# Last-64-row items of an attention and spectral-mix kernel moved from the end to the middle of the tail

## The chip, the cores and the metric

One Trainium2 chip, one of its cores. The metric is device time in microseconds. The kernel before took 428.51 us as the median of 7 runs (427.82 to 429.5). Beside these there is one profiled execution, which took 429.14 us; the instructions that the profile shows span 427.4 us of it. All times below with one or two decimals and no other source are places in that span, counted from its start.

## What is computed

Eight batches, eight heads, 576 positions and head size 64. Four heads use a local causal window of 32 positions, four a strided mask. The attention result, read as 576 rows of 512 columns per batch, then goes through a spectral mix and a residual layer:

```python
scores = np.where(masks[None], scale * np.matmul(q, k.transpose(0, 1, 3, 2)), -1e9)
attn = softmax(scores)
x = np.matmul(attn, v)                       # then laid out as (8, 576, 512)
X = np.fft.rfft(x, axis=1)
Yr = einsum('bmd,mde->bme', Xr, w_r) - einsum('bmd,mde->bme', Xi, w_i)   # 64 modes
Yi = einsum('bmd,mde->bme', Xr, w_i) + einsum('bmd,mde->bme', Xi, w_r)
u = x + np.fft.irfft(Yr + 1j * Yi, n=S, axis=1)
return u + np.maximum(u @ w_ch, 0.0)         # (8, 576, 512) in float32, 9.44 MB
```

## The kernel before, in words

The first two stages do attention (strided heads, then local heads), with the spectral products of the 64 modes woven in while their weights stream in from HBM. The weights come through transfers that the GpSimd queue issues (line 186), and that stream fills most of the span. The program writes the order of the instructions out by hand: each engine executes its instructions in the order of the code.

The change lies in the tail, which begins once the last weights have landed (about 391 us). The output is produced there by 18 *items*. An item is a pair (batches, t). For t from 0 to 3 it holds two batches and, of each, 128 rows of the output (every second row of the first 256 or of the next 256 rows). For t = 4 it holds four batches and, of each, the last 64 rows (512 to 575); the first batch of each pair lies on partitions 0 to 63 of a tile, the second on partitions 64 to 127. Every item has 512 KB of output. In the kernel before, items 0 to 15 have t < 4, and items 16 and 17 are the two with t = 4 (line 976).

For each item k the tail does, in this order:

- `v_early(k)` (line 987): two matmuls with the identity bring the kept product of the residual layer into PSUM. `u_early(k)` (line 992) does the same with the kept rows.
- `new_rows` (line 1001): matmuls over 32 rows that add what the last spectral group brings, from `zzs` to the v half and from `yys` to the u half. An item with t < 4 takes two of them for each half, an item with t = 4 takes four, each for 64 rows.
- `v_done(k)` (line 1013): ScalarE writes the ReLU of the v half to `rl`.
- `u_done(k)` (line 1020): VectorE adds the u half and `rl` into an output tile `osb`. Then a transfer stores it: at line 1028, one for an item with t < 4, on the queue of SyncE; at line 1031, one for each batch of an item with t = 4, also on SyncE's queue, except that odd batches of the last item are stored from ScalarE's queue.

The loop at line 1067 runs the v half of item k beside the u half of item k-1. At k = 8 it first runs `spec_z(3, 1, held)` (line 736), four matmuls whose result `zzs[1]` the items with batches 4 to 7 need, and a copy of it by ScalarE. `pieces(k)` cuts the ReLU, the addition and the store of item 0 in two. `osb` tiles rotate over five buffers, those that held the weights. PSUM has three two-bank buffers `p` and one `u`; an even item's u half uses `p`, an odd one's `u`.

Of the kernel before, what the change touches and what calls it, by code (L numbers as in the profile page):

```python
# [56 lines left out]
def kernel(  # L57
# [10 lines left out]
    nc = tc.nc  # L68
# [17 lines left out]
    def psum(kind, half=False, pair=False):  # L86
        if pair:
            return pss[kind].tile([128, 2, 512], FP, tag=kind, name=kind)
        if half:
            return pss[kind].tile([128, 1024], F16, tag=kind, name=kind)  # L90
        return pss[kind].tile([128, 512], FP, tag=kind, name=kind)
# [146 lines left out]
    def normalise(val, den, n, pieces, dst):  # L238
        rec = pin.tile([128, 8], FP, tag="rec", bufs=4, name="rec")
        nc.vector.reciprocal(out=rec[0:n, 0:pieces], in_=den)  # L240
        nc.vector.tensor_tensor(  # L241
            out=dst,
            in0=val.rearrange("p h (q c) -> p h c q", c=4),
            in1=rec[0:n, 0:pieces]
            .to_broadcast((n, pieces, 64))
            .rearrange("p h (q c) -> p h c q", c=4),
            op=AluOp.mult,
        )

    def act_copy(out, in_):  # L250
        nc.scalar.activation(out=out, in_=in_, func=ACTF.Copy)  # L251
# [481 lines left out]
    def spec_z(g, bq, zp):  # L733
        for e in range(4):
            lhs = YS["YT"][:, e, g, ds(8 * bq, 8), :].rearrange("p x m -> p (x m)")
            nc.tensor.matmul(
                zp, lhs, w_chs["n"][:, e, :], start=(e == 0), stop=(e == 3)
            )
# [228 lines left out]
    for n, i in enumerate([3, 5, 7] + list(range(8, 21))):  # L967
        b, t = n // 2, n % 2 * 2
# [4 lines left out]
    items = []  # L973
    for P0 in (0, 2):
        items += [((2 * P, 2 * P + 1), t) for t in range(4) for P in (P0, P0 + 1)]
    items += [(range(b, b + 4), 4) for b in (0, 4)]
    LAST = len(items) - 1
    vps, ups, rls, osbs = {}, {}, {}, {}

# [4 lines left out]
    def v_early(k):  # L984
        vps[k] = psum("p", pair=True)
        for j, r in enumerate(own(items[k], v0s, v0h)):
            nc.tensor.matmul(vps[k][:, j], idn, r, start=True, stop=False)  # L987

    def u_early(k):
        ups[k] = psum(("p", "u")[k % 2], pair=True)  # L990
        for j, r in enumerate(own(items[k], xos, xoh)):
            nc.tensor.matmul(ups[k][:, j], idn, r, start=True, stop=False)  # L992

    def new_rows(k, acc, spectra):
        bs, t = items[k]
        for j, b in enumerate(bs):
            q = ds(32 * (b % 4), 32)
            o, cols = acc[:, j % 2], out_cols(t)
            if t == 4:
                o = acc[ds(64 * (b % 2), 64), j // 2]  # L1000
            nc.tensor.matmul(  # L1001
                o, A3[q, cols], spectra[b // 4][q], start=False, stop=True
            )

    def pieces(k):
        return [slice(0, 1), slice(1, 2)] if k == 0 else [slice(0, 2)]

    def v_done(k):
        rl = ptr.tile([128, 2, 576], FP, tag=("xT", "rl")[k // 2 % 2], bufs=2, name="rl")
        rls[k] = rl[:, :, 0:DM]  # L1010
        vp = vps.pop(k)
        for j in pieces(k):
            nc.scalar.activation(out=rls[k][:, j], in_=vp[:, j], func=ACTF.Relu)  # L1013

    def u_done(k):
        bs, t = items[k]
        up, rl = ups.pop(k), rls.pop(k)
        osb = pw.tile([128, 2, DM], FP, tag="w", name="osb")
        for j in pieces(k):
            nc.vector.tensor_tensor(  # L1020
                out=osb[:, j], in0=up[:, j], in1=rl[:, j], op=AluOp.add
            )
            if t < 4:
                rows = out[:, ds(128 * (t - t % 2), 256), :].rearrange(
                    "b (p i) e -> p b i e", i=2
                )
                own_b = slice(bs[0] + j.start, bs[0] + j.stop)
                nc.sync.dma_start(rows[:, own_b, t % 2], osb[:, j])
        if t == 4:
            for b in bs:  # L1030
                (nc.scalar if b % 2 and k == LAST else nc.sync).dma_start(
                    out[b, ds(512, 64), :], osb[ds(64 * (b % 2), 64), b // 2 % 2, :]
                )

    flush()
# [26 lines left out]
    for k in range(2):  # L1062
        if k:
            u_early(k)
        new_rows(k, ups[k], yys)
        u_done(k)
    for k in range(2, LAST + 2):
        if k == 8:
            held = psum("p", pair=True)[:, 0]
            spec_z(3, 1, held)  # L1070
            act_copy(zzs[1], held)
        if k <= LAST:
            v_early(k)
        if k > 2:
            u_early(k - 1)
        if k <= LAST:
            new_rows(k, vps[k], zzs)
        if k > 2:
            new_rows(k - 1, ups[k - 1], yys)
        if k <= LAST:  # L1080
            v_done(k)
        if k > 2:
            u_done(k - 1)
# [31 lines left out]
```

## Time and profile before

| | |
|---|---|
| median of 7 runs | 428.51 us |
| profiled execution, its own time | 429.14 us |
| span of its instructions | 427.4 us |
| last weights landed, tail begins | about 391.3 us |
| first store issued (line 1028) | 397.09 us |
| stores of 512 KB on SyncE's queue (line 1028) | 15, and 2 of 256 KB |
| stores of 128 KB (line 1031) | 6 on SyncE's queue, 2 on ScalarE's |
| one store at line 1028 holds its queue | 0.34 to 0.39 us |
| one store at line 1031 holds its queue | 0.53 to 0.78 us |
| addition of a whole item on VectorE (line 1020) | 1.22 us |
| ReLU of a whole item on ScalarE (line 1013) | 1.02 us |

The span is the time from the first to the last instruction of the profiled execution. A row of the timeline gives the start in us, the duration in us, the engine, the line and what is written and read; in brackets stands how long the engine was idle before it and what ended that. A row of the table by windows gives, for a stretch of the span, the busy time of each engine, the granted TensorE clock, the mean busy share of the 16 DMA engines and the GB/s that they moved.

### The profile page before, as it was taken

The page shows a single profiled execution, that of the slowest core. Times are in us where ns is not written, and L with a number is a line of the kernel's source. Part 1 is how long each engine was busy: PE and PEld are TensorE (multiplying, and loading weights), DVE is VectorE, ACT ScalarE, POOL GpSimd, SP SyncE. Part 2 cuts the span into 40 slices and gives each one's busy share as a digit, 9 for nine tenths or more (in the row PEclk, how much of TensorE's full clock was granted, in tenths as well). Part 3 has the DMA queues.
Part 4 walks back from the last instruction along what each step waited for, and adds up shares of the span by engine and source line. Part 5 has one row for each costly group of instructions (what it writes and reads, how often), then busy time and mean ns, then how long its engine had stood idle before and what let it go on. Part 6 is the DMA issues. An engine that isn't in the chain of part 4 may idle for free.

```text
span 427.4 us, 9767 instructions
## 1 busy us (share of the span) xinstructions
PE 346.5 (81%) x4167; PEld 208.5 (49%) x4167; DVE 235.0 (55%) x466; ACT 218.3 (51%) x390; POOL 110.7 (26%) x196
## 2 busy tenths in 40 slices
PE   2987878779999698789678689867979777998993
PEld 2866767654666365556433344434445323544330
DVE  3788778851455154356203347754675452663884
ACT  1687778643656456566542424422442543553872
POOL 8332333322423222222221322222222222110000
PEclk9999899957999899999985989999899987998997
DMA  8999999999999999999999999999999999994698
GB/s 153 209 211 213 214 211 213 211 211 211 215 214 212 212 214 213 214 215 214 210 215 212 213 214 214 211 213 214 213 213 214 213 214 213 213 213 91 255 353 276
DMA packets 30938, 91.62 MB, mean 214 GB/s; under 512 B 4464, under 2 KB 5232, under 8 KB 30896
## 3 DMA queue, kind: packets, MB, share of 16 engines
q0 software_dynamic: 25168, 81.28, 96.1%
q1 hardware_dynamic: 5136, 9.39, 6.2%
q8 instruction: 32, 0.52, 0.5%
q10 hardware_dynamic: 592, 0.35, 0.3%
q14 instruction: 10, 0.08, 0.0%
HBM read 162.83 MB, written 9.44 MB: 403 GB/s over the span
## 4 chain that ended last, share of the span: by engine, by line
DMA 56%; PE 22%; DVE 12%; ACT 4%; issue 3%; POOL 0%; DVEq 0%; POOLq 0%; ACTq 0%
DMA wt<-in_moe_w_i_dram 40%; DMA wt<-in_moe_w_r_dram 10%; DMA ring<-in_v_dram 5%; PE y L597 3%; DVE xb L241 3%; DVE kz L283 2%; PE p L987 2%; PE sc L532 2%; ACT X L251 2%; PE p L1001 1%; DVE yy L752 1%; PE tp L276 1%; DVE rec L240 1%; PE sc L717 1%; PE p L992 1%
## 5 line engine op out<-in xcount | busy, mean ns | idle before, releaser
L597 PE MATMUL y<-wt,X 128*32 128x512 f16 (+1 forms) x448 | 68.1, 416 | 22.7 <-DMA wt<-in_moe_w_i_dram 22.7
L186 POOL DMA_DIRECT2D wt<-in_moe_w_r_dram x59 | 34.6, 587 | 118.7 <-PE y L597 36.3
L186 POOL DMA_DIRECT2D wt<-in_moe_w_i_dram x60 | 35.4, 589 | 75.0 <-DMA wt<-in_moe_w_i_dram 51.6
L597 PEld LDWEIGHTS <-X 128*32 128x32 f16 (+1 forms) x448 | 27.9, 139 | 40.9 <-DMA wt<-in_moe_w_i_dram 21.1
L726 ACT ACTIVATE v<-sc 128x512 f16<-128x512 f32 x32 | 19.1, 597 | 47.9 <-PE sc L717 47.9
L727 DVE COPY xo<-tp 128x512 f16<-128x512 f16 x32 | 22.1, 691 | 37.3 <-PE tp L725 37.3
L241 DVE TENSOR_TENSOR xb<-av,rec 90x256 f16<-90x256 f32 (+2 forms) x80 | 36.0, 450 | 2.8
L717 PE MATMUL sc<-w_cp,xT 128*128 128x512 f16 x128 | 36.2, 404 | 1.4 <-DVE xT L690 1.4
L489 ACT ACTIVATE PL<-sc 128x480 f16<-128x480 f32 (+1 forms) x48 | 26.9, 578 | 20.3 <-PE sc L475 19.9
L240 DVE RECIPROCAL rec<-av 90x4 f32<-90x4 f32 (+2 forms) x80 | 14.6, 183 | 39.5 <-PE av L504 28.9
L251 ACT ACTIVATE yr<-y 128x512 f16<-128x512 f32 x28 | 16.7, 597 | 35.1 <-PE y L597 34.0
L961 DVE TENSOR_TENSOR xo<-p,xo 128x1024 f16<-128x1024 f32 x16 | 19.6, 1225 | 20.1 <-PE p L760 20.0
L420 DVE COPY qT<-tp 128x576 f16<-128x576 f16 x16 | 11.9, 752 | 32.9 <-PE tp L413 32.9
L251 ACT ACTIVATE v<-p 128x1024 f16<-128x1024 f32 x16 | 16.4, 1023 | 21.5 <-PE p L760 21.5
L378 ACT ACTIVATE PL<-sc 90x360 f16<-90x360 f32 (+1 forms) x48 | 22.8, 490 | 7.0 <-PE sc L371 6.4
L251 ACT ACTIVATE v<-tp 128x640 f16<-128x640 f16 (+1 forms) x24 | 19.0, 807 | 11.7 <-PE tp L447 9.0
L413 PE MATMUL tp<-cI_s,ring 64*64 64x64 f16 x864 | 22.8, 198 | 2.1 <-DVE qT L420 1.7
L459 PE MATMUL sc<-cMl_s,cI_s 128*128 128x480 f16 (+1 forms) x48 | 18.7, 391 | 5.3 <-ACT PL L489 3.7
L276 PE MATMUL tp<-cI_s,ring 72*128 72x72 f16 x256 | 15.4, 207 | 8.6 <-DMA ring<-in_v_dram 7.0
L251 ACT ACTIVATE kz<-tp 64x360 f16<-64x360 f16 (+1 forms) x32 | 18.9, 592 | 6.1 <-PE tp L413 5.2
L413 PEld LDWEIGHTS <-ring 64*64 64x64 f16 x864 | 18.0, 112 | 8.3 <-issue 4.2
L1013 ACT ACTIVATE rl<-p 128x1024 f32<-128x1024 f32 (+1 forms) x19 | 18.4, 979 | 5.9 <-PE p L1001 3.3
(142 smaller groups left out, 742.1 us busy)
## 6 DMA issues: line engine op xcount, KB each, us to landing
wt<-in_moe_w_i_dram POOLq DMA_DIRECT2D x60, 512.0 KB, 18.5
wt<-in_moe_w_r_dram POOLq DMA_DIRECT2D x59, 512.0 KB, 18.0
out_dram<-osb SPq DMA_DIRECT2D x15, 512.0 KB, 3.2
ring<-in_v_dram POOLq DMA_DIRECT2D x8, 288.0 KB, 13.3
ring<-in_q_dram POOLq DMA_DIRECT2D x8, 288.0 KB, 13.6
ring<-in_k_dram POOLq DMA_DIRECT2D x8, 288.0 KB, 13.1
ring<-in_v_dram POOLq DMA_DIRECT2D x3, 512.0 KB, 14.6
ring<-in_q_dram POOLq DMA_DIRECT2D x3, 512.0 KB, 14.8
```

The lines of the kernel that those rows point to most:

```text
L186: nc.gpsimd.dma_start(dst, rows)
L241: nc.vector.tensor_tensor(out=dst, in0=val.rearrange("p h (q c) -> p h c q", c=4), in1=rec[0:n, 0:pieces] .to_broadcast((n, pieces, 64)) . ...
L251: nc.scalar.activation(out=out, in_=in_, func=ACTF.Copy)
L276: nc.tensor.transpose(tp[:, ds(72 * i, 72)], qn[:, ds(128 * (a + i), 128)], idn[0:72, 0:72],)
L378: nc.scalar.activation(out=PS[0:n, ds(POFF[t], 4 * n)], in_=scp[0:n, 0 : 4 * n], func=ACTF.Exp, scale=SCALE,)
L413: nc.tensor.transpose(tp[ds(64 * hp, 64), ds(64 * i, 64)], qn[ds(64 * hp, 64), ds(64 * (9 * g + i), 64)], idn[ds(64 * hp, 64), ds(64 * hp, ...
L489: nc.scalar.activation(out=dst, in_=src, func=ACTF.Exp, scale=SCALE)
L597: nc.tensor.matmul(yp[ds(a, 32), :], Xh[half][pr, c].rearrange("p b r (h m) -> p (b r h) m", h=2)[:, :, mm % 32], wt[pr, XC[c], :], start= ...
L717: nc.tensor.matmul(vp, xT[:, ch], w_chs["cp"][:, ch, :], start=(ch == 0), stop=(ch == 3),)
L726: nc.scalar.activation(out=v0, in_=vp, func=ACTF.Copy)
L727: nc.vector.tensor_copy(out=xo.rearrange("p (h q c) -> p h q c", h=2, c=4), in_=tp[:, 0:512].rearrange("p (h c q) -> p h q c", h=2, c=4),)
L961: nc.vector.tensor_tensor(out=xo, in0=up[:, 0:n], in1=xo, op=AluOp.add)
```

## The change

The item of batches 0 to 3 with t = 4 becomes item 8, and that of batches 4 to 7 becomes item 13. The other items keep their order, so that the last item, 17, is now one of two batches with t = 3. The four matmuls of `spec_z(3, 1, held)` are run at k = 9 instead of 8, ahead of the first item that holds batches 4 to 7. The last item's ReLU, addition and store are cut in two pieces, as item 0's were. An item with t = 4 is stored by two transfers on SyncE's queue instead of four: one takes the two batches on partitions 0 to 63, the other the two on partitions 64 to 127, 256 KB each. ScalarE's queue issues no store any more.

```diff
-    items += [(range(b, b + 4), 4) for b in (0, 4)]
+    items.insert(8, (range(0, 4), 4))
+    items.insert(13, (range(4, 8), 4))
...
     def pieces(k):
-        return [slice(0, 1), slice(1, 2)] if k == 0 else [slice(0, 2)]
+        return [slice(0, 1), slice(1, 2)] if k in (0, LAST) else [slice(0, 2)]
...
         if t == 4:
-            for b in bs:
-                (nc.scalar if b % 2 and k == LAST else nc.sync).dma_start(
-                    out[b, ds(512, 64), :], osb[ds(64 * (b % 2), 64), b // 2 % 2, :]
+            for b in bs[0:2]:
+                nc.sync.dma_start(
+                    out[b : bs[-1] + 1 : 2, ds(512, 64), :].rearrange("j p e -> p j e"),
+                    osb[ds(64 * (b % 2), 64)],
                 )
...
     for k in range(2, LAST + 2):
-        if k == 8:
+        if k == 9:
             held = psum("p", pair=True)[:, 0]
             spec_z(3, 1, held)
             act_copy(zzs[1], held)
```

## Prediction

> **What bounds the kernel now.** I read the page's slices first, to see what is busy in the tail, then the timeline of the tail, then the table by windows there. The slices:
>
> ```profile
> PE   2987878779999698789678689867979777998993
> DMA  8999999999999999999999999999999999994698
> GB/s 153 209 211 213 214 211 213 211 211 211 215 214 212 212 214 213 214 215 214 210 215 212 213 214 214 211 213 214 213 213 214 213 214 213 213 213 91 255 353 276
> ```
>
> The last three slices (10.7 us each) are the tail. In the next to last the stores move 353 GB/s at a share of 9 and in the last the rate falls to 276, still at a share of 8. The chain of waits puts TensorE on the path until 420.2, because each step of it is followed through matmuls. So I ask whether the stores keep up. One-microsecond windows around the middle of the tail, and one long window after it (the last two numbers of a row are DMA share and GB/s):
>
> ```profile
> 408.00:409.00 1.00, 1.00 (x8) 0.31 (x4) 0.93 (x2) 0.73 (x2) 0.00 (x0) 1.00 0.53 197
> 409.00:410.00 1.00, 1.00 (x8) 0.40 (x8) 0.93 (x2) 0.73 (x2) 0.00 (x0) 1.00 0.79 299
> 410.00:421.00 11.00, 10.05 (x67) 2.94 (x65) 9.96 (x9) 7.77 (x8) 0.00 (x0) 1.00 1.02 377
> ```
>
> From about 409.2 to 421 the DMA engines never rest: 377 GB/s at a share of 1.02. An item is 524,288 bytes, so it takes them 1.39 us, while TensorE brings one each 1.296 us (for instance line 987 starts at 406.88, 408.18, 409.47). The stores are the slower side. What sets the end is when the DMA engines last ran dry, and how long the bytes after that take. They ran dry for (1 - 0.53) + (1 - 0.79) = 0.68 us, about 408.53 to 409.21. The timeline says why:
>
> ```profile
> 404.42 1.04 PE L736 MATMUL p<-w_ch,YT 128*128 128x512 f16 x4
> 405.60 0.59 PE L987 MATMUL p<-v,cI_s 128*128 128x512 f16 x2
> 407.08 1.23 DVE L1020 TENSOR_TENSOR osb<-u,rl 128x1024 f32<-128x1024 f32 x1 [1.24 <-PE u L1001]
> 408.33 0.37 SPq L1028 DMA_DIRECT2D out_dram<-osb  x1
> ```
>
> The four matmuls of line 736 delay item 7: its addition starts 1.24 us late, its store is issued at 408.33 and its bytes start 0.88 us after that. From 409.21 on there are nine items of 1.39 us (7 to 15), to 421.7. Then come the eight stores of 128 KB, on 64 partitions each:
>
> ```profile
> 421.75:423.00 1.25, 0.00 (x0) 0.00 (x0) 0.00 (x0) 0.00 (x0) 0.00 (x0) 0.80 0.90 200
> 423.50:426.00 2.50, 0.00 (x0) 0.00 (x0) 0.00 (x0) 0.00 (x0) 0.00 (x0) 0.50 0.92 276
> 426.00:426.50 0.50, 0.00 (x0) 0.00 (x0) 0.00 (x0) 0.00 (x0) 0.00 (x0) 0.50 0.00 0
> ```
>
> Here the engines are busy (0.90, 0.92) and yet slow: 200 GB/s while the first two stores (batches 0 and 1) go one after the other, 276 once several are in line, on two queues. The last byte moves just before 426.0; the remaining 1.4 us are its confirmation and the closing steps.
>
> **The change part by part, worked against this profiled execution.**
>
> *Two stores instead of four, SyncE's queue alone.* The issues at the end looked expensive:
>
> ```profile
> 420.54 3.93 SPq L1031 DMA_DIRECT2D out_dram<-osb  x6
> 421.67 1.22 ACTq L1031 DMA_DIRECT2D out_dram<-osb  x2
> ```
>
> Six issues hold the queue of SyncE from 420.54 to 424.47. In the middle, two issues of 0.37 to 0.78 us per item fit into the 1.3 us between two items, and the stores behind them wait for the DMA engines anyway, so this costs nothing there. If that cover is gone, it is (2 x 0.78 - 1.3), 0.3 us once. ScalarE's two issues disappear at a time when it had nothing left to do: 0.
>
> *The last item with t = 3, cut in two.* Its first half is issued about 0.6 us earlier, but it waits in line. Counting from the v half of item 9 at 407.08 (next part) with steps of 1.296 us, and 1.62 or 1.52 us where an item of t = 4 takes part, item 17's v half starts at 418.2, item 16's addition ends near 421.0, and the two pieces of 0.69 us end near 422.3. Its second half could move from 423.2 on; by the sum below its turn comes at 425.5. Some 2.2 us of cover, hence 0. The same cover hides the extra time on TensorE, which is the same four matmuls per half as before, only earlier.
>
> *Line 736 one step later.* Now item 7 is not delayed. TensorE is free for k = 8 at 404.42. The v half of a t = 4 item makes this iteration 1.62 us (line 987 at 415.96 and 417.58 for k = 16 now), and there the addition starts 1.79 us after that start (417.75). So item 7's addition starts at 406.21, its store leaves at 407.45, and its bytes can start at 408.33, before item 6 is through at 408.53: the old gap closes. The new one opens behind item 7, at 408.53 + 1.39 = 409.92. Line 736 runs from 406.04 to 407.08. Then come item 9's v half, item 8's u half (it needs the PSUM buffer of item 8's ReLU, which is done at 406.9) and the four row matmuls. For k = 17 the addition follows 1.71 us after line 987 (417.58 to 419.29), so item 8's starts at 408.79, ends at 410.01, the store leaves at 410.03. With 0.88 us to its bytes: 410.91. The 128 KB stores may start slower: batch 0's, issued at 420.54, moves from about 421.7, 1.18 us, though the line of stores ahead hides part of that; this end would be 411.2. I take 410.95, nearer to the ordinary store, whose access pattern has the same two dimensions.
>
> *The rest after this point:* eight full items, 8 x 1.39 = 11.1 us, to 422.05, and two t = 4 items.
>
> *What a t = 4 item costs as two stores of 64 partitions.* The trace has no 256 KB store of this form. Bounds: 1.39 us at the full 377 GB/s; 524,288 / 200 = 2.62 us at the rate of batches 0 and 1. Between them lies the rate of the stores that stood in line, 276 GB/s: 1.90 us. Item 13 meets a line of waiting stores, so I take 1.9. Item 8 meets idle engines, and its first half runs alone until the second has been issued: 2.2. Sum 4.1, bounds 2.8 and 5.2. [...] stores of both halves overlap once their issues are early enough. [...] I stay with the measured rates, since the middle of the tail has early issues[...].
>
> **Sum.** Last byte at 422.05 + 4.1 = 426.15, against 426.0: +0.15 us. [...] What is won at the end (the eight slow stores take 4.3 us now, the two items took 2.8 at full rate) is paid in the middle, because the stores there have no slack, and the gap behind line 736 grows from 0.68 to 1.03 us. The profiled execution (429.14, with 427.4 between first and last instruction) lies 0.6 above the median of the runs, within their spread; the difference is carried to the median: 428.51 + 0.15, about 428.7, and 427.55 for the new span if it is profiled alike.
>
> **Rivals.**
>
> *Half stores flow at full rate (faster).* [...] For: 377 GB/s in the window 424.0 to 424.5, with both kinds in flight. Against: 184 in the next one. Then 1.39 each: 422.05 + 2.78 = 424.83, -1.2 us, 427.3. It is a gain beyond 0.2% (0.86 us, about what a measurement of this kernel can tell from no change) from 1.54 us per item, 340 GB/s. That the stores don't bind at all, and the earlier last issue counts in full (last bytes from 423.2 to 423.9, -2.1), is possible only if the share of 1.02 misleads; I leave 2 in 100 for it, within this rival.
>
> *Half stores serialize (slower).* The place is items 8 and 13, the price 2.62 us each, and nothing after them has slack to win it back: 422.05 + 5.24 = 427.3, +1.3 us, 429.8. For: the 200 GB/s[...]. Against: the 276. [...]
>
> *A new wait behind the slower stores.* An output tile is used again five items later, 6.5 us of production. Item 8's store would end near 413.2, item 13's addition starts near 416; item 9's near 414.5, item 14's near 417.3. More than 2 us of room; at 2.6 us per item still 2. I give it no time of its own.
>
> **How the numbers follow.** Within 0.2%: 0.56, at 428.7. Faster: 0.17, at 427.3 to 427.6. Slower: 0.27, at 429.4 to 429.8[...]. The range 427.5 to 429.8[...].
>
> **What would show each step.** In the changed profile: item 7's store near 407.45 and item 8's near 410.0; DMA engines dry from 409.9 to 410.9 and not after that; under 300 GB/s in the windows that hold items 8 and 13, with a share near 1; 377 GB/s up to the end, which is at full rate; last byte near 426.15. The prediction is wrong if the windows of items 8 and 13 show 377 GB/s (then 427.3) or 200 (then 429.8), if the gap at 410 is much longer than 1 us, or if DMA shares near the end fall below 1 because TensorE has become the later side.

## The result: 0.43% slower, outside the range

The changed kernel takes 430.79 us as a median (429.12 to 431.92), the kernel before beside it 428.66; the ratio is 1.0043, 95% interval 1.0035 to 1.0052, about 1.8 us (1.5 to 2.2; the two medians differ by 2.1). The forecast was 428.7, its range ended at 429.8.

The profiled execution of the changed kernel took 432.3 us, longer than any of the others, and has a span of 430.5 us, 3.1 more than the one before. Part of that lies ahead of the changed lines: after the last weights TensorE's granted clock stayed at 0.50 until about 398 instead of 395, and the tail started later. One microsecond shows it, first before the change and then after it (the clock is the third number from the end):

```profile
396.00:397.00 1.00, 1.00 (x6) 0.21 (x4) 0.79 (x3) 1.00 (x3) 0.00 (x0) 1.00 0.00 0
```

```profile
396.00:397.00 1.00, 1.00 (x7) 0.19 (x6) 0.76 (x2) 0.38 (x1) 0.00 (x0) 0.50 0.00 0
```

So I compare the tails alone: *T* is the time from the fourth addition (item 2's, in steady state for both) to the end of the last output packet in the trace's DMA records. Before, it runs from 399.44 to 425.99, 26.55 us; after, from 400.72 to 428.98, 28.26 us. The difference is 1.71 us. It lies within the interval of the measured loss, so the tail accounts for the loss as closely as the runs can tell. From item 2 on the changed execution stands 1.28 us later on the clock, so 1.28 has to be added to the prediction's places.

The stores first, in the table by windows of the changed kernel (the last two columns are the DMA share and GB/s):

```profile
410.00:411.00 1.00, 1.00 (x8) 0.30 (x6) 1.00 (x1) 0.62 (x1) 0.00 (x0) 1.00 1.00 387
411.00:412.00 1.00, 1.00 (x8) 0.31 (x4) 0.90 (x2) 0.78 (x1) 0.00 (x0) 1.00 0.17 62
412.00:413.00 1.00, 1.00 (x8) 0.41 (x8) 0.93 (x2) 0.73 (x2) 0.00 (x0) 1.00 0.41 90
413.00:414.00 1.00, 1.00 (x9) 0.27 (x7) 0.93 (x2) 0.73 (x2) 0.00 (x0) 1.00 0.96 178
414.00:415.00 1.00, 1.00 (x8) 0.25 (x6) 1.00 (x1) 0.84 (x1) 0.00 (x0) 1.00 1.00 272
415.00:420.00 5.00, 5.00 (x34) 1.64 (x31) 4.05 (x5) 3.40 (x4) 0.00 (x0) 1.00 1.03 381
420.00:423.00 3.00, 1.84 (x11) 0.48 (x9) 2.93 (x4) 1.78 (x3) 0.00 (x0) 1.00 0.98 264
423.00:428.00 5.00, 0.00 (x0) 0.00 (x0) 0.48 (x1) 0.00 (x0) 0.00 (x0) 0.73 1.03 390
428.35:429.00 0.65, 0.00 (x0) 0.00 (x0) 0.00 (x0) 0.00 (x0) 0.00 (x0) 0.50 0.06 22
```

One sees four things. The gap in front of item 8 is (1 - 0.17) + (1 - 0.41) = 1.42 us, against 0.68 before. While the half stores of items 8 and 13 move, the engines are busy (0.96 to 1.00) and slow (178 to 272 GB/s): in the packet records a packet of 2,048 bytes took 167 ns on the mean from 412.6 to 414.0, and 86 ns from 415.5 to 420.0. The ordinary stores between and behind them run at 381 and 390. And at the end, from 428.35 to 428.98, the share is 0.06: one engine of 16 is still moving its packets. The trace records 16 landings of each store, as many as there are engines. They lie within 0.25 us for the lower half of item 8, but 1.29 us apart for its upper half, and more than 1.2 us apart for every store after that; of the last store, one lands 0.67 us behind the other 15.

The work behind it, in the timeline of the changed kernel:

```profile
407.33 1.04 PE L736 MATMUL p<-w_ch,YT 128*128 128x512 f16 x4
408.75 0.37 SPq L1029 DMA_DIRECT2D out_dram<-osb  x1
410.00 1.23 DVE L1021 TENSOR_TENSOR osb<-p,rl 128x1024 f32<-128x1024 f32 x1 [1.27 <-PE p L1002]
411.25 0.69 SPq L1032 DMA_DIRECT2D out_dram<-osb  x1
```

Item 7's store leaves at 408.75 (forecast 407.45 + 1.28 = 408.73), item 8's addition starts at 410.00 (410.07), its first store leaves at 411.25 (411.31). The work went as worked out; the stores did not.

### The profile page after: what moved, and what is told of

Its sections match the earlier page's. It is cut to its first block, busy times and chain, and to the rows that moved or that the text cites. A ratio compares the mean times of both kernels' runs of the same rounds, so it can differ in the third digit from the quotient of the medians.

```text
span 430.5 us, 9767 instructions
## 1 busy us (share of the span) xinstructions
PE 349.3 (81%) x4167; PEld 208.5 (48%) x4167; DVE 234.8 (55%) x467; ACT 218.2 (51%) x391; POOL 110.8 (26%) x196
## 4 chain that ended last, share of the span: by engine, by line
DMA 47%; PE 31%; DVE 13%; ACT 3%; issue 3%; POOL 1%; DVEq 0%; POOLq 0%
DMA wt<-in_moe_w_i_dram 31%; DMA wt<-in_moe_w_r_dram 11%; PE y L597 7%; DMA ring<-in_q_dram 5%; PE sc L717 3%; DVE xb L241 3%; DVE kz L283 2%; PE p L988 2%; ACT X L251 2%; PE tp L413 2%; PE p L1002 1%; PE sc L532 1%; PE sc L459 1%; PE y L532 1%; DVE yy L752 1%
## 5 line engine op out<-in xcount | busy, mean ns | idle before, releaser
L597 PE MATMUL y<-wt,X 128*32 128x512 f16 (+1 forms) x448 | 70.3, 427 | 17.2 <-DMA wt<-in_moe_w_i_dram 17.0
L717 PE MATMUL sc<-w_cp,xT 128*128 128x512 f16 x128 | 37.8, 419 | 1.9 <-DVE xT L690 1.9
```

What stands on the lines that cost most here:

```text
L597: nc.tensor.matmul(yp[ds(a, 32), :], Xh[half][pr, c].rearrange("p b r (h m) -> p (b r h) m", h=2)[:, :, mm % 32], wt[pr, XC[c], :], start= ...
L717: nc.tensor.matmul(vp, xT[:, ch], w_chs["cp"][:, ch, :], start=(ch == 0), stop=(ch == 3),)
```

## The experiments

Three theories stood at first. PLACE: the half stores (64 partitions in a row) cost more in the middle than at the end. WORK: the moved matmuls and line 736 cost it. FORM: two large halves in turn overlap less than four small ones. Later two more: START, that the late and slow beginning of item 8 counts most; and REACH, that it counts which 64 partitions a store takes: that one from 64 neighbouring partitions is slow and one from 64 alternating partitions is not. All ratios are to the kernel before on the same chip, with 95% intervals; T is from one profiled execution of each; two pairs of kernels at the end of the table that should have the same tail agree in T within 0.06 us.

| kernel | ratio | T, us |
|---|---|---|
| before | 1 | 26.55 |
| changed | 1.0043 (1.0035 to 1.0052) | 28.26 |
| two stores, order of before | 1.0006 (0.9991 to 1.0021) | 26.75 |
| moved, four stores | 1.0016 (0.9998 to 1.0033) | 27.45 |
| work moved, half stores at the end | 1.0014 (1.0001 to 1.0027) | 27.09 |
| half stores moved, work not | 1.0032 (1.0020 to 1.0044) | 27.30 |
| changed, line 736 at k = 8 | 1.0050 (1.0030 to 1.0069) | 28.41 |
| changed, upper half on GpSimd's queue | 1.0051 (1.0034 to 1.0068) | 28.19 |
| all items t < 4 in two halves | 1.0258 (1.0231 to 1.0284) | 36.91 |
| the same, even and odd partitions | 1.0094 (1.0068 to 1.0121) | 30.35 |
| changed, even and odd partitions | 0.9990 (0.9978 to 1.0002) | 25.98 |
| order of before, even and odd partitions | 0.9979 (0.9970 to 0.9988) | 25.33 |
| the same with the right output | 0.9986 (0.9975 to 0.9997) | 25.28 |
| the same, moved | 0.9991 (0.9977 to 1.0005) | 25.92 |

**Two stores instead of four, nothing moved.**

```diff
-            for b in bs:
-                (nc.scalar if b % 2 and k == LAST else nc.sync).dma_start(
-                    out[b, ds(512, 64), :], osb[ds(64 * (b % 2), 64), b // 2 % 2, :]
-                )
+            for b in bs[0:2]:
+                nc.sync.dma_start(
+                    out[b : bs[-1] + 1 : 2, ds(512, 64), :].rearrange("j p e -> p j e"),
+                    osb[ds(64 * (b % 2), 64)],
+                )
```

> The order of the kernel before; only the stores of the two items with t = 4 (still the last two) are two transfers of 256 KB on SyncE's queue instead of four of 128 KB. Three theories for the 1.0043 of the changed kernel: PLACE (stores from 64 partitions cost more in the middle of the tail than at its end), WORK (the moved matmuls, additions and line 736 cost it), FORM (two large halves one after the other overlap less than four small ones). FORM expects the two items' bytes to take near 5.2 us instead of 4.3: ratio 1.002 or more. PLACE and WORK expect 0.999 to 1.001.

1.0006, T 0.2 us longer. At the end the number of transfers makes no difference that can be told: FORM alone is not the cause.

**Moved, but four stores.**

```diff
-            for b in bs[0:2]:
+            for b in bs:
                 nc.sync.dma_start(
-                    out[b : bs[-1] + 1 : 2, ds(512, 64), :].rearrange("j p e -> p j e"),
-                    osb[ds(64 * (b % 2), 64)],
+                    out[b, ds(512, 64), :], osb[ds(64 * (b % 2), 64), b // 2 % 2, :]
                 )
```

> The changed kernel, but each item with t = 4 is stored by four transfers of 128 KB on SyncE's queue, lower and upper half in turn. FORM expects most of the loss to go: ratio 1.001 or less. PLACE and WORK expect it to stay at 1.0035 to 1.005; if the queue is held longer by four issues, a little more.

1.0016, T +0.9: half of the loss is gone, so in the middle the two large halves are worse than four small ones. Neither forecast was met. The late engine is gone: the 16 landings of the last store lie within 0.26 us, against 1.34 us in the changed kernel. Both PLACE and FORM have a part.

**Work and stores apart.** Two kernels exchange the places of the stores' forms and leave the order of the work. In both, `u_done` takes (batches, t) from a list of its own:

```diff
-        bs, t = items[k]
+        bs, t = stored[k]
```

> The changed kernel's work in the changed order, but the forms of the stores stay where they were before the change: items 8 and 13 are stored by one transfer over 128 partitions each (to the rows of the last two items), and the last two items by two half stores each (to the last 64 rows). The output has its rows exchanged. WORK expects 1.003 to 1.005, as the changed kernel. PLACE expects what the kernel with two stores at the end gives, within 0.001. FORM the same as PLACE.

1.0014, T +0.54, of which 0.2 is what the two stores at the end cost anyway.

> The other half of it: the work in the order before the change, but items 8 and 13 are stored by two half stores each (to the last 64 rows) and the last two items by one transfer over 128 partitions each. The output has its rows exchanged. PLACE expects 1.003 to 1.005 and in the profile slow windows (near 200 GB/s) after items 8 and 13. WORK expects 0.999 to 1.001. FORM expects what the kernel with two stores at the end gives.

1.0032, T +0.75, with the slow windows where the half stores now are:

```profile
411.00:413.00 2.00, 2.00 (x15) 0.62 (x14) 1.86 (x2) 1.46 (x3) 0.00 (x0) 1.00 0.80 186
413.00:416.00 3.00, 3.00 (x19) 1.02 (x18) 2.85 (x3) 2.46 (x3) 0.00 (x0) 1.00 1.00 322
419.00:422.00 3.00, 1.79 (x16) 0.37 (x14) 2.45 (x3) 1.18 (x2) 0.00 (x0) 1.00 0.96 295
```

Both are what PLACE expected. The stores carry more of the loss than the work; neither carries it all, and 0.34 and 0.75 add up to 1.09 of the 1.71. The other 0.6 comes only when both are moved, and these two runs don't say why. WORK as the whole is out.

**Line 736 back at k = 8.**

```diff
-        if k == 9:
+        if k == 8:
```

> The changed kernel with line 736 left at k = 8, so that item 7 and not item 8 is the one it delays. START (the first half store of item 8 comes late to idle engines, and with 1.34 us to its first byte instead of 0.88) expects 0.5 to 0.7 us back: from the fourth addition to the last byte 27.6 to 27.8 us instead of 28.26, ratio near 1.003. If only the half stores' rate counts, 28.2 us and 1.004.

Nothing came back: 1.0050, T 28.41. START's forecast failed, but the trial doesn't rule START out, for the engines ran dry no less than before. The gap only split in two, one in front of item 7 and one in front of item 8, as the windows of this kernel show:

```profile
406.00:407.00 1.00, 1.00 (x9) 0.20 (x6) 0.81 (x1) 0.43 (x2) 0.00 (x0) 1.00 0.76 285
407.00:408.00 1.00, 1.00 (x8) 0.31 (x4) 0.77 (x1) 0.84 (x1) 0.00 (x0) 1.00 0.28 104
408.00:409.00 1.00, 1.00 (x8) 0.41 (x8) 0.90 (x2) 0.55 (x1) 0.00 (x0) 1.00 1.02 385
409.00:410.00 1.00, 1.00 (x8) 0.31 (x7) 0.93 (x2) 0.73 (x2) 0.00 (x0) 1.00 0.29 80
```

Together they are 0.24 + 0.72 + 0.71 = 1.67 us, 0.25 more than the changed kernel's 1.42, and T is 0.15 longer. Behind item 7's store the engines run dry again, because item 8's first half needs 1.34 us from its issue to its first packet.

**The two halves on two queues.**

```diff
-                nc.sync.dma_start(
+                (nc.gpsimd if b % 2 else nc.sync).dma_start(
```

> The changed kernel with the two half stores of an item with t = 4 on two queues: lower half on SyncE's, upper half on GpSimd's, which has nothing else to do here. SERIAL (the two halves stand one behind the other[...]) expects each of the two items to cost 0.5 to 1 us less, since both halves move at once: 26.5 to 27.3 us from the fourth addition to the last byte, ratio 1.000 to 1.002. If a half store is slow by itself, whatever moves beside it, it stays at 28 us and 1.004.

1.0051, T 28.19. This trial says little on the question it was made for: in its packet records the upper half of item 8 starts about 1.4 us after the lower one (412.67 against 411.29), so they hardly moved side by side.

**All items in halves, in a row and alternating.** The suspected cost, taken eight times over, and a control with the same transfers from other partitions:

```diff
-                nc.sync.dma_start(rows[:, own_b, t % 2], osb[:, j])
+                for h in (slice(0, 64), slice(64, 128)):
+                    nc.sync.dma_start(rows[h, own_b, t % 2], osb[h, j])
```

> The kernel before, but each of the 16 items with t < 4 is stored by two transfers of 256 KB, partitions 0 to 63 and 64 to 127, one after the other on SyncE's queue. It multiplies the suspected cost by eight. [...] Half stores that overlap at 276 GB/s (1.9 us per item): 6 to 8 us more, 1.015 to 1.02. Only the bookkeeping of more transfers: below 1.005.

In the control the slices are `slice(0, 128, 2)` and `slice(1, 128, 2)`.

> As the kernel with all items in halves, with the same number, size and queue of transfers, but one takes the even and one the odd partitions. If a half store is slow [...], this one is not slow: 0.999 to 1.005. If it is slow because it has 64 partitions, or by its size or its issue, it is as slow as the other.

1.0258 and 1.0094. A long window in each, first the one in a row, then the alternating one:

```profile
404.00:424.00 20.00, 15.98 (x95) 4.70 (x93) 12.25 (x10) 11.51 (x12) 0.00 (x0) 1.00 0.86 267
```

```profile
404.00:420.00 16.00, 14.72 (x91) 4.64 (x88) 12.40 (x11) 11.04 (x12) 0.00 (x0) 1.00 1.02 378
```

Same number, size, queue and shape of transfers; 267 GB/s against 378, which is the rate of the full stores. So 64 partitions are not slow here, 64 neighbouring ones are. (The rows of the output that a store writes change along with its partitions here; in the next experiment they do not.) The control's own 0.94% is above its forecast. Its trace shows where much of it lies: at the end SyncE waits 2.4 us for an earlier store to land before it issues the third of its 128 KB stores, at 426.88, and the DMA engines run dry. The first line gives who waited, for what, and the us in total, the times and the longest wait; the second is a window:

```profile
SPq L1032 <- DMA out_dram<-osb: 2.4, 1, 2.4
```

```profile
427.00:428.00 1.00, 0.00 (x0) 0.00 (x0) 0.00 (x0) 0.00 (x0) 0.00 (x0) 0.50 0.03 6
```

I take that for a cost of the number of stores and not of their partitions, which these two runs do not show by themselves; the remainder was not taken apart. In a row, 1.0258 lies above the forecast of 1.015 to 1.02 for half stores that overlap at 276 GB/s. The long window moved 267 GB/s, not the 200 that the kernel before shows for batches 0 and 1.

**The changed kernel with alternating partitions.** The decisive one; it changes nothing but which 64 partitions a store takes:

```diff
-            for b in bs[0:2]:
+            for h in range(2):
                 nc.sync.dma_start(
-                    out[b : bs[-1] + 1 : 2, ds(512, 64), :].rearrange("j p e -> p j e"),
-                    osb[ds(64 * (b % 2), 64)],
+                    out[bs[0] + h : bs[-1] + 1 : 2, ds(512, 64), :].rearrange("j p e -> p j e"),
+                    osb[h:128:2],
                 )
```

> The changed kernel, order and number of transfers untouched, but the two stores of an item with t = 4 take the even and the odd partitions instead of the lower and the upper 64. Rows of the last 64 come out exchanged. REACH ([...] this is the whole of the slow windows and of the engines that end late) expects the slow packets (mean 130 to 170 ns) and the late engine to be gone, only the later start to stay: 26.7 to 27.3 us from the fourth addition to the last byte instead of 28.26, ratio 1.000 to 1.0015. If the size or number of the transfers in the middle is at fault, nothing changes: 28.2 us, 1.004.

0.9990, T 25.98: more than the whole loss is gone, and more than REACH expected: its 26.7 to 27.3 did not count that the kernel before pays for its half stores too, at its end. The profile's answer on the store line, first of the changed kernel, then of this one (how long an issue held the queue, in ns, min/median/max, and the first and last start; then the time from issue to landing):

```profile
L1032 SPq DMA_DIRECT2D out_dram<-osb x4: 595/651/1542, 411.3 to 419.1; - x4
DMA to landing us min/median/max: 3.3/4.2/5.1
```

```profile
L1032 SPq DMA_DIRECT2D out_dram<-osb x4: 601/609/692, 408.8 to 416.6; - x4
DMA to landing us min/median/max: 2.5/2.5/2.5
```

And its windows over item 8's time and over the rest:

```profile
408.00:409.00 1.00, 1.00 (x9) 0.28 (x7) 0.90 (x2) 0.40 (x2) 0.00 (x0) 1.00 0.79 299
409.00:410.00 1.00, 1.00 (x9) 0.23 (x7) 1.00 (x1) 0.83 (x1) 0.00 (x0) 1.00 0.01 4
410.00:411.00 1.00, 1.00 (x12) 0.34 (x8) 0.93 (x2) 0.90 (x1) 0.00 (x0) 1.00 0.83 309
410.20:412.90 2.70, 2.70 (x18) 0.81 (x16) 2.45 (x2) 2.13 (x3) 0.00 (x0) 1.00 1.01 374
412.90:423.90 11.00, 6.52 (x40) 2.02 (x38) 7.32 (x7) 5.01 (x6) 0.00 (x0) 1.00 1.01 374
```

No slow window is left. The 16 landings of the last store lie within 0.15 us, so the late engine came with the neighbouring halves too. What stays is the gap in front of item 8, 0.21 + 0.99 + 0.17 = 1.37 us, and its 1.34 us to the first packet, which is the same from neighbouring and from alternating partitions.

**The same stores at the end.** The store lines of the last diff in the order of before.

> The order of the kernel before, the stores of the last two items as two transfers of even and of odd partitions. Rows of the last 64 come out exchanged. REACH expects the 1.3 us that the slow packets cost at the end to go: 25.2 to 25.6 us from the fourth addition to the last byte instead of 26.55, ratio 0.996 to 0.998. Otherwise as the kernel with two half stores at the end, 26.75 us and 1.0005.

0.9979, T 25.33, as REACH expected. With this the four kernels make a square: the neighbouring halves cost 26.55 - 25.33 = 1.22 us in the old order (its four half stores against two alternating ones) and 28.26 - 25.98 = 2.28 in the new one. The order itself, without the half stores, costs 25.98 - 25.33 = 0.65. The change's 1.71 is 0.65 for the order and 1.06 for what the half stores cost more in the middle. (With two neighbouring halves per item at the end, T 26.75, they cost 1.42 there.) The 0.65 is about what the gap grew by, from 0.68 to 1.37 us; with full stores in the middle, above, the order cost 0.34, so I put part of it, an estimate, on the later start of a store from 64 partitions (1.34 us from issue to first packet against 0.88).

**With the right output.** To make the alternating stores correct, the two batches of a pair are laid on even and odd partitions in the items with t = 4:

```diff
-        x4 = x4s[b // 2][:, :, ds(64 * (b % 2), 64)]
+        x4 = x4s[b // 2].rearrange("p c (r j) -> p c j r", j=2)[:, :, b % 2]
...
+        if t == 4:
+            for j in range(2):
+                q = ds(64 * j, 64)
+                nc.tensor.matmul(
+                    acc[:, j], A4[q], spectra[bs[0] // 4][q], start=False, stop=True
+                )
+            return
```

`A4` holds the last 64 columns of `A3` with zeros in every second column, so that one matmul over 64 rows adds both batches. The earlier spectral groups use two such matrices in `rows_of`.

> As the one before, with the right output: the two batches of a pair lie on even and odd partitions in the items with t = 4, by matrices with zeros in every second column, so that two batches' 32 rows are added by one matmul of 64 rows. Order of the kernel before. REACH expects 25.1 to 25.6 us, ratio 0.996 to 0.998; a little less work for TensorE at the end.

0.9986 (0.9975 to 0.9997), T 25.28: by a little faster than the kernel before, and faster than the changed one. T is as forecast, the ratio just above its forecast. The end of its profile, where the kernel before fell to 200 GB/s:

```profile
409.00:421.00 12.00, 10.36 (x60) 3.07 (x58) 10.93 (x9) 8.12 (x8) 0.00 (x0) 1.00 1.02 379
421.00:424.00 3.00, 0.00 (x0) 0.00 (x0) 0.00 (x0) 0.00 (x0) 0.00 (x0) 0.78 0.96 355
```

> The same layout in the order of the changed kernel. REACH expects that the place then matters only by the start behind line 736: 26.3 to 26.9 us from the fourth addition to the last byte, ratio 0.999 to 1.0005, between the right-output kernel with the old order and the changed kernel.

0.9991, T 25.92, below the forecast of 26.3 to 26.9, and 0.64 us behind the unmoved one, as in the square above; the ratios of the two can't be told apart.

## Why the prediction was wrong

Its sum was 422.05 for everything but the two items, plus 4.1 for them, 426.15 against 426.0. By its own steps, in tails:

- *The stores bind, not TensorE.* Right. The share is 1.03 at 381 GB/s between the items, and no change of the work's order alone made 1.71 us.
- *Places of the work.* Right within 0.1 us, as the timeline above shows. Item 7's old gap closed (share 1.02 from 408.0 to 410.9).
- *The start of item 8.* Mis-sized. Forecast 0.88 us from the issue to the first packet, with an upper end of 1.18; measured 1.34 (411.25 to 412.59), and the same with alternating partitions. The step took the ordinary store's value because the access pattern has two dimensions as well. The gap became 1.42 us instead of 1.03: +0.39.
- *What a half-store item costs.* This is the step that failed. It took 1.9 and 2.2 us, 4.1 in all, from the 276 GB/s of the last stores before. From item 8's first packet to the last one are 428.98 - 412.59 = 16.39 us; less the eight full items, 11.1, that leaves 5.3. Of these 0.65 are the one engine that is late at the end, which no step foresaw. The other 4.64 are 0.54 more than forecast. The 276 were measured with stores of 128 KB in turn from lower and upper half, on two queues; the changed kernel has 256 KB from one half and then 256 KB from the other, on one queue. The moved kernel with four stores, which alternates more finely, has no late engine and T 0.8 us shorter. Stored from alternating partitions, the same items move at 374 GB/s and the step costs nothing: 2.28 us come back. The sum 0.15 + 0.39 + 0.54 + 0.65 is 1.73, against 1.71. The square says the same in other terms: the order was forecast at 0.35 (the gap, 1.03 less 0.68) and cost 0.65; the stores of the two items were forecast to win 0.2 (4.1 us against 4.3 for the eight small ones) and lost 1.06.
- *Which partitions a store takes.* No step of the sum had it. The alternating stores ran at 374 to 378 GB/s; windows of the changed kernel with stores in a row show 178 to 272. That the partitions of a store decide is shown (T 28.26 against 25.98 us with nothing else changed); why they do is not seen in any trace. The 429.4 at the lower end of the slower side was an estimate of mine that no run shows.
- *The rivals.* "Half stores serialize" had the place and, at 5.2 us, nearly the price, this last in part by luck: of the measured 5.3, 0.65 is the late engine, which it did not foresee. Its 200 GB/s are near what a single item shows (178 from 413 to 414), but not what a long line of half stores does (267). It ended at 429.8 since the later start was not in it. It had 0.27. "Half stores flow at full rate" is what happened with alternating partitions (374 to 378 GB/s). The wait for an output tile, which had been given no time, did not come in the changed kernel.

Why a half store leaves the engines out of step is open: the packet records do not say which engine moved a packet.

## What to carry to other kernels

When stores bind, ask of each one which partitions it takes, and not only how many bytes and transfers it has: here 64 alternating partitions stored at full rate (374 to 378 GB/s) and 64 neighbouring ones did not (178 to 272 in the changed kernel). Where a slow transfer stands matters as well: two neighbouring halves per item cost 1.42 us at the end and 2.28 in the middle, where no time was free beside them and where they also came back as a late engine at the end. A rate read from one form of transfer should not be carried to another without both bounds; look first at whether the row is of the same form.

## What the runs showed of the hardware beyond this

- From issue to first packet a full store of 128 partitions took 0.88 us, a 64-partition one of two rows each 1.34 us, from neighbouring and alternating partitions alike, and one of a single row each, with no store ahead of it, 1.17 us (in the moved kernel with four stores). The one of two rows also holds its queue longer (0.60 to 0.70 us against 0.37).
- While the stores are backed up, SyncE's issues take longer: up to 1.54 us for one in the changed kernel. The DMA engines stay busy meanwhile (share 0.98 to 1.03 from 415 to 428), so I take it to cost nothing here.
- In the profiled executions of the 14 kernels, TensorE's granted clock after the pause behind the last weights stood at 0.50 for 6.8 us once (the changed kernel), for 3.4 us in seven (the kernel before among them) and not at all in six. From the last weight packet to the fourth addition it took 9.2 us, 8.3 to 8.5 and 7.2. So executions of kernels that are nearly the same up to there differ by up to 2 us ahead of the tail, which is why T is used here beside the medians.
- In both kernels a packet of 16 KB on a queue that the profile calls "instruction" (0.96 us at 399.8 before, 0.93 us at 400.7 after) goes with one landing of item 0's second store that comes 2.0 us behind the other 15. By item 7 this is down to 0.02 and 0.08 us, and no such packet follows, so the late engine at the end is another matter.
